# Outputs scaled in place of weights in four attention pairs, with an earlier second pair and two compose tiles

## The chip, the cores and the metric

One core of a Trainium2 chip runs the kernel. TensorE multiplies matrices, VectorE (DVE in the rows), ScalarE (ACT) and GpSimd (POOL) work on tiles, and SyncE (SP) issues most transfers. The metric is the device time of one launch in microseconds, less is better.

## The reference

Causal attention with a forget gate over 4 batches, 8 heads, 576 positions and 64 dimensions; then a dense feed-forward layer; then a layer in which each of the 2304 tokens goes to one of 8 experts. The change is in the attention and in the preparation of the dense layer's weights.

```python
scores = scale * np.matmul(q, k.transpose(0, 1, 3, 2))
log_f = np.log(np.clip(f, 0.0001, 1.0))
cum = np.cumsum(log_f, axis=-1)
decay = cum[:, :, :, None] - cum[:, :, None, :]
scores = np.where(causal, -1000000000.0, scores + decay)
scores = scores - np.max(scores, axis=-1, keepdims=True)
attn = np.exp(scores)
attn = attn / (np.sum(attn, axis=-1, keepdims=True) + 1e-09)
return np.matmul(attn, v).astype(np.float32)
...
h = x @ w_in
g = np.where(pos, h, np.where(neg, 0.0, (h + beta) ** 2 / (4.0 * beta)))
return (g @ w_out).astype(np.float32)
```

The dense layer's weights come in as 64-bit floats.

## The kernel before, in words

**Attention.** Two heads of a batch make a pair, and there are 16 pairs, 0 to 15. A pair has five units, taken in the order 4, 3, 2, 1, 0. Units 3 to 0 are blocks of 128 queries against the 512 to 128 keys they may see, both heads apart; unit 4 is the last 64 queries of both heads together against all 576 keys. For a unit, TensorE forms scores in a score bank (`SR` or `SRx`). In pairs 0 to 3 (`i < NSUM`) it also adds the running decay by products with `cum` or `parts`; in later pairs the decay comes as a mask `cm`, `cl`. Then for each head, in `head`:

- VectorE masks the scores, writes them to a tile `P` and takes the maximum (`tensor_tensor_reduce`, L588).
- ScalarE takes the exponential and its sum (L593), the sum going to a column of `st`.
- VectorE adds 1e-9 to the unit's sums (L598) and takes reciprocals (L600).
- GpSimd scales the weights in `P` by the reciprocal (L604).
- TensorE turns `P` in blocks of 128 into a bank `T` (L618; L616 for the last block), and ScalarE or VectorE copies it to `pt` or `pu` (L638, L636).

When both heads of units 3 to 0 are there, `weighted` multiplies them with the values into a bank `X` (L658), the value products, and ScalarE copies `X` to `xT` (L665). `weighted_last` does unit 4 (`U`, L711). `xT` goes to DRAM in `xs`. For the first four pairs its first 256 tokens also become the first block of the dense layer (`px0h`, `px0l`, in `first_block`), whose products can start when all four are there.

**Loads.** `load` brings the query and the key block of a pair (`rawq`, `rawk`, two tiles each) by four transfers on the SP queue, and VectorE turns each (L448). Pair 0 loads at once; every later pair waits for `sums_there`, the running sums of the forget gate.

**Weights.** The dense layer runs in two halves of the features. The weights of the first half (`wa`) come in 16 pieces of 128x512, a piece of `w_in` and one of `w_out` by turns. `float64_piece` makes each piece in a float32 tile `wx` and writes a high and a low part: an absolute value on ScalarE (L829), a maximum with a guard value (L830), three integer steps (L832, L834, L836) on VectorE, a cast on ScalarE (L840) and a subtraction on GpSimd (L841). One tile `wx` serves all pieces (`wx_b`), so a piece starts when the one before it is through.

**The dense layer** of the first half (`half0`) forms hidden banks (`hp`, L886), gates them on ScalarE, VectorE and GpSimd, and sums the second product in `accp` (L1020). It is mixed with attention from the end of pair 3 on: blocks 0 and 1 need batch 0 alone.

**Order.** The instructions of each engine are put in order ahead of time by a planner (`Order`), which lets the parts of the program run as coroutines against estimated costs. What was ready in its plan goes out by priority; the order is then fixed on each engine, and semaphores keep it right. Where TensorE has nothing in the plan during the first four pairs, `keep_warm` puts in products of `ident` with itself (`warm`, L735), which compute nothing that is used.

Of the kernel before, what the change touches and what calls it, by code (L numbers as in the profile page):

```python
# [18 lines left out]
P = 128  # L19
# [21 lines left out]
FIRST_WEIGHTS = [6000.0 + 2700.0 * n for n in range(5)] + [20500.0 + 5200.0 * n for n in range(11)]  # L41
PACE = 8500.0
WARM_FROM, WARM = 1500.0, 0.6

# [151 lines left out]
def act(n, fn, prio=5.0, more=0.0):  # L196
    return Use("ACT", 155 + n / 1.2 + more, fn, prio)
# [27 lines left out]
def kernel(  # L225
# [100 lines left out]
    for b in range(B):  # L326
        for n in range(b * S // TB, ((b + 1) * S - 1) // TB + 1):
            xs_ok[n].n += NPAIR
    raws, qkt, cms, vs, pt, pt4, xts = {}, {}, {}, {}, {}, {}, {}

# [60 lines left out]
    def load(i, n):  # L391
# [13 lines left out]
        g = yield (raw_b[n], 1)  # L405
        if i:
            yield sums_there
        t = yield dma(P * S * 6, lambda: put({"q": q, "k": k}[n], n), 4 if i else 0.5, k=4)
        raws[i, n] = (t, g)
# [109 lines left out]
    def unit(i, c, started):  # L519
# [47 lines left out]
        yield cm_ok[i, c]  # L567
        st = ap.tile([P, 8], F32, tag="st", name=f"st{i}_{c}", bufs=10)
        summed, scaled = Event(len(heads)), Event()
        left = Event(len(heads))  # L570
# [6 lines left out]
    def head(i, j, c, p, gp_, bank, st, summed, scaled, left):  # L577
# [8 lines left out]
        else:  # L586
# [4 lines left out]
        done(left)  # L591
        done(read_ok[i, c])
        yield act(w, lambda: nc.scalar.activation(pw, pw, AF.Exp, bias=st[:, n:n + 1], scale=-1.0,  # L593
                                                  accum_out=st[:, 2 + n:3 + n]), 1, 330)
        done(summed)
        if n == 0:
            yield summed
            yield Use("DVE", 150, lambda: nc.vector.tensor_scalar(  # L598
                st[:, 4:4 + k], st[:, 2:2 + k], 1e-9, None, ALU.add), 0)
            yield Use("DVE", 150, lambda: nc.vector.reciprocal(st[:, 6:6 + k], st[:, 4:4 + k]), 0)  # L600
            done(scaled)
        else:
            yield scaled
        yield pool1(w, lambda: nc.gpsimd.tensor_scalar(pw, pw, st[:, 6 + n:7 + n], 1.0, ALU.mult,  # L604
                                                       ALU.mult), 0)
        yield pt_ok[i, j]
# [33 lines left out]
        done(last_ok[i] if c == 4 else heads_ok[i])  # L640

    def weighted(i):

# [3 lines left out]
        xT = xts[i] = ap.tile([P, S], F32, tag="xT", name=f"xT{i}", bufs=2)  # L647
        go(weighted_last(i))
        vt, gr = vs[i]
        yield heads_ok[i]  # L650
# [12 lines left out]
        for j in range(2):  # L663
            give(pt_b, pt.pop((i, j))[1])
        yield act(512, lambda: nc.scalar.copy(xT[:, :512], X), 0)  # L665
        give(x_b, g)
# [74 lines left out]
    def attention():  # L741
# [23 lines left out]
    wr_b, wx_b, xl_b, t1_b, t2_b, x2_b, h_b, g_b, acc_b = (  # L765
        Buffers(2), Buffers(1), Buffers(1), Buffers(1), Buffers(1), Buffers(1), Buffers(1), Buffers(2), Buffers(0))

# [33 lines left out]
    def float64_weights(W, src_a, src_b, times, prio):  # L801
# [5 lines left out]
        for fc in range(NF):  # L807
            cs = slice(P * fc, P * fc + P)
            for src, hi, lo, ok in ((a[:, :, cs], ah[:, :, cs], al[:, :, cs], W.ok[0][fc]),
# [5 lines left out]
                n += 1  # L815

    def float64_piece(g, src, hi, lo, ok, name, prio):
        def put():
# [8 lines left out]

        x = fp.tile([P, DM], I32, tag="wx", name=name + "x", bufs=1)
        yield act(DM, lambda: nc.scalar.activation(f32(x), f32(hw), AF.Abs), prio)  # L829
        yield dve(DM, lambda: nc.vector.tensor_scalar(f32(x), f32(x), MIN64, None, ALU.max), prio,  # L830
                  True)
        yield dve(DM, lambda: nc.vector.tensor_scalar(  # L832
# [845 lines left out]

    W0 = Weights(wp1, "wa")
    with tc.manual_schedule():  # L1680
        go(attention())
        go(float64_weights(W0, w_in[:, :FH], w_out[:FH], FIRST_WEIGHTS, 0.8))
        go(phases())
        o.run()
        assert last_out.n == 0
# [38 lines left out]
```

## Time and profile before

| | |
|---|---|
| median of 3 runs | 861.24 us (859.62 to 863.11) |
| the profiled execution | 862.92 us, span 861.3 us |
| mean granted TensorE clock | 0.995 |
| busy: PE, DVE, ACT, POOL | 98%, 54%, 42%, 36% of the span |

The span runs from the first to the last instruction. Shares of busy time are means over the span. In the first ten of 40 slices DVE shows 5 to 9 tenths and in the last ones 1 to 2, so they are read by stretch.

### The profile page before, as it was taken

Reading aid. Unit: us, or ns where it says so; the run is one execution under the profiler, and the core shown is the slowest. Engines: PE = TensorE matmul, PEld = TensorE weight load, DVE = VectorE, ACT = ScalarE, POOL = GpSimd, SP = SyncE. Lnnn points to the kernel's source line nnn. Section 1 sums busy time; section 2 is a strip of 40 time slices with the busy share of each in tenths; the row PEclk is TensorE's granted clock in tenths of the full one; section 3 lists DMA queues with packets and bytes.
Section 4 is the critical chain, followed back from the end, with each engine's and each line's share of the span. In section 5 each row is a group of like instructions: output and inputs, shape, how many; then the busy total and the mean of one; then the engine's idle time right before and its main releaser. Section 6 shows DMA issues by size and latency. Waiting matters only on the chain.

```text
span 861.3 us, 14317 instructions
## 1 busy us (share of the span) xinstructions
PE 840.4 (98%) x5000; PEld 672.7 (78%) x5000; DVE 463.9 (54%) x1112; ACT 361.9 (42%) x845; POOL 306.4 (36%) x407
## 2 busy tenths in 40 slices
PE   9999998999999999999999999999999999999995
PEld 7665776787777798887788888888998888887684
DVE  6797977665555538766766344466544522212111
ACT  5677766665656635444344242323333212112110
POOL 3576876565455434544343122312210033000000
PEclk9999999999999999999999999999999999999998
DMA  7998666564323236225331135653431111721220
GB/s 139 184 183 182 167 159 145 139 135 108 113 67 118 78 103 134 74 75 171 117 127 49 73 123 159 189 191 123 147 123 73 50 50 50 263 103 50 98 74 25
DMA packets 152264, 101.91 MB, mean 118 GB/s; under 512 B 102866, under 2 KB 121810, under 8 KB 152192
## 3 DMA queue, kind: packets, MB, share of 16 engines
q1 hardware_dynamic: 149024, 96.22, 40.7%
q0 software_dynamic: 2832, 4.22, 1.7%
q8 instruction: 40, 0.66, 0.3%
q10 hardware_dynamic: 336, 0.56, 0.2%
q14 instruction: 32, 0.26, 0.1%
HBM read 76.86 MB, written 24.49 MB: 118 GB/s over the span
## 4 chain that ended last, share of the span: by engine, by line
PE 83%; DVE 7%; POOL 2%; issue 2%; DMA 2%; ACT 2%; SPq 0%; ACTq 0%; DVEq 0%; POOLq 0%
PE hm L886 12%; PE hr L886 12%; PE hp L886 9%; PE accp L1020 6%; PE accr L1020 6%; PE accBr L1020 6%; PE accm L1032 6%; PE accBm L1032 6%; PE SR L538 4%; PE T L618 4%; PE X L658 4%; PE gt L1236 1%; PE U L711 1%; PE SR L533 1%; PE T_None L618 1%
## 5 line engine op out<-in xcount | busy, mean ns | idle before, releaser
L908 POOL TENSOR_TENSOR glr<-gr,ghr 128x512 fp32r<-128x512 f32 x36 | 48.3, 1341 | 141.7 <-PE accBr L1020 69.1
L604 POOL TENSOR_SCALAR P<-P,st 128x512 f32<-128x512 f32 (+3 forms) x128 | 76.9, 615 | 38.8 <-DVE st L600 25.4
L886 PE MATMUL hr<-rx,wb 128*128 128x512 f32 (+1 forms) x384 | 90.1, 368 | 0.2 <-DVE rx L872 0.2
L886 PE MATMUL hm<-mx,wm 128*128 128x512 f32 (+1 forms) x336 | 87.0, 379 | 0.0
L593 ACT ACTIVATE P<-P,st 128x512 f32<-128x512 f32 (+3 forms) x128 | 71.4, 559 | 32.9 <-DVE st L588 31.8
L917 DVE SCALAR_TENSOR_TENSOR glm<-hm,ghm 128x512 fp32r<-128x512 f32 x36 | 24.8, 689 | 103.5 <-PE accBm L1032 68.4
L916 ACT ACTIVATE ghm<-hm 128x512 fp32r<-128x512 f32 x36 | 21.6, 599 | 132.9 <-PE accBm L1032 120.6
L886 PEld LDWEIGHTS hr<-rx,wb 128*128 128x128 f32 x384 | 65.5, 188 | 14.0 <-DVE rx L872 0.6
L886 PEld LDWEIGHTS hm<-mx,wm 128*128 128x128 f32 x336 | 61.0, 188 | 14.9 <-issue 3.4
L908 POOL TENSOR_TENSOR glp<-gp,ghp 128x512 fp32r<-128x512 f32 x36 | 49.8, 1383 | 55.1 <-ACT ghp L907 48.2
L1020 PE MATMUL accp<-ghp,wa 128*128 128x256 f32 (+1 forms) x384 | 68.8, 307 | 0.0
L588 DVE CUSTOM_DVE_ANT_0 P<-SR,cm 128x512 f32<-128x512 f32 (+3 forms) x96 | 45.1, 484 | 24.8 <-PE SR L538 22.5
L1020 PEld LDWEIGHTS accp<-ghp,wa 128*128 128x128 f32 x384 | 53.9, 190 | 5.3 <-issue 2.2
L618 PE MATMUL T<-ident,P 128*128 128x128 f32 x320 | 52.5, 278 | 3.5 <-POOL P L604 2.9
L638 ACT COPY pt<-T 128x512 f32<-128x512 f32 (+2 forms) x96 | 35.3, 391 | 35.9 <-PE T L618 35.2
L902 DVE SCALAR_TENSOR_TENSOR gr<-tr 128x512 f32<-128x512 f32 x36 | 25.9, 721 | 42.6 <-POOL glr L908 31.7
L618 PEld LDWEIGHTS T<-ident,P 128*128 128x128 f32 x320 | 36.7, 141 | 14.9 <-POOL P L604 6.5
L538 PE MATMUL SR<-kt,qt 64*128 64x384 f32 (+3 forms) x224 | 44.9, 478 | 3.0 <-DVE st L588 2.9
L1020 PE MATMUL accr<-ghr,wb 128*128 128x512 f32 (+1 forms) x160 | 47.0, 375 | 0.0
L1020 PE MATMUL accBr<-ghr,wb 128*128 128x512 f32 (+1 forms) x160 | 46.5, 372 | 0.0
L1032 PE MATMUL accm<-wm,ghm 128*128 128x512 f32 x144 | 46.2, 394 | 0.0
L1032 PE MATMUL accBm<-wm,ghm 128*128 128x512 f32 x144 | 45.8, 392 | 0.0
(345 smaller groups left out, 1864.3 us busy)
## 6 DMA issues: line engine op xcount, KB each, us to landing
cm<-rows SPq DMA_DIRECT2D x24, 256.0 KB, 4.3
rawq<-in_q_dram SPq DMA_DIRECT2D x64, 72.0 KB, 3.5
rawk<-in_k_dram SPq DMA_DIRECT2D x64, 72.0 KB, 3.2
xs<-xT SPq DMA_DIRECT2D x16, 288.0 KB, 2.2
x2n<-nat SPq DMA_DIRECT2D x18, 256.0 KB, 2.6
war<-in_moe_w_in_dram SPq DMA_DIRECT2D x8, 512.0 KB, 4.3
war<-in_moe_w_out_dram SPq DMA_DIRECT2D x8, 512.0 KB, 5.0
rawv<-in_v_dram SPq DMA_DIRECT2D x32, 128.0 KB, 2.6
```

Of the source, the lines that this page charges most:

```text
L538: nc.tensor.matmul(bank[:, j, :w], qt[p, P * c:P * c + P], kt[p, :w], start=True, stop=i >= NSUM)
L588: yield dve(w + 80, lambda: nc.vector.tensor_tensor_reduce(out=pv_, in0=so, in1=m, scale=-0.125, scalar=3e38, op0=ALU.add, op1=ALU.min, ac ...
L593: yield act(w, lambda: nc.scalar.activation(pw, pw, AF.Exp, bias=st[:, n:n + 1], scale=-1.0, accum_out=st[:, 2 + n:3 + n]), 1, 330)
L604: yield pool1(w, lambda: nc.gpsimd.tensor_scalar(pw, pw, st[:, 6 + n:7 + n], 1.0, ALU.mult, ALU.mult), 0)
L618: nc.tensor.transpose(T[:, P * n:P * n + P], p[:, P * kb:P * kb + P], ident)
L638: yield act(n, lambda: nc.scalar.copy(dh, src), 0)
L658: nc.tensor.matmul(X[D * j:D * j + D, P * kb:], vt[:, kb, j], pt[i, j][0][:, 512 * kb:512 * kb + 512 - P * kb], start=(kb == 0), stop=(kb ...
L886: nc.tensor.matmul(oo, a[:, c, cs], x[c], start=(ip == 0 and c == 0), stop=(ip == 2 and c == KC - 1))
L902: yield dve(n, lambda: nc.vector.scalar_tensor_tensor(g, t, 0.5, t, ALU.min, ALU.mult), 2)
L908: yield pool2(n, lambda: nc.gpsimd.tensor_tensor(gl, g, f32(gh), ALU.subtract), 1)
L1020: nc.tensor.matmul(acc[d][:, :w], b[:, fc, P * d:P * d + P], g, start=(fc == 0 and ip == 0 and (not narrow or d % 2 == 0)), stop=(fc == NF ...
L1032: nc.tensor.matmul(acc[a * (4 // na)], g[:, P * a:P * a + P], b[:, fc], start=(fc == 0 and ip == 0), stop=(fc == NF - 1 and ip == 2))
```

## The change

In pairs 0 to 3, units 3 to 0 are no longer scaled as weights. Their sums go to a tile `tot` of the pair (a column for each unit and head). When all eight are there, `shares` adds 1e-9, takes the reciprocals in one instruction each, and TensorE spreads them by eight products with `ident` into a bank `hR` that has the layout of `X`. `weighted` then lets ScalarE copy `hR` to `xT`, and VectorE multiplies `X` with it. Unit 4 and all later pairs stay as they were. Pair 1 loads when pair 0's key block has landed, ahead of the running sums. `wx_b` has two tiles until the first half's weights are made, the second of them in the pool of the attention; and nine of these pieces take their guard maximum on GpSimd.

```diff
-        if i:
+        if i == 1:
+            yield raw_ok[0, "k"]
+        elif i:
             yield sums_there
-        t = yield dma(P * S * 6, lambda: put({"q": q, "k": k}[n], n), 4 if i else 0.5, k=4)
+        t = yield dma(P * S * 6, lambda: put({"q": q, "k": k}[n], n),
+                      4 if i > 1 else 0.5, k=4)
...
+        late_sum = i < NSUM and c < 4
+        total = sums_of[i][:, c, n:n + 1] if late_sum else st[:, 2 + n:3 + n]
         yield act(w, lambda: nc.scalar.activation(pw, pw, AF.Exp, bias=st[:, n:n + 1], scale=-1.0,
-                                                  accum_out=st[:, 2 + n:3 + n]), 1, 330)
+                                                  accum_out=total), 1, 330)
         done(summed)
-        if n == 0:
+        if late_sum:
+            done(all_summed[i])
+        elif n == 0:
...
-        yield pool1(w, lambda: nc.gpsimd.tensor_scalar(pw, pw, st[:, 6 + n:7 + n], 1.0, ALU.mult,
-                                                       ALU.mult), 0)
+        if not late_sum:
+            yield pool1(w, lambda: nc.gpsimd.tensor_scalar(pw, pw, st[:, 6 + n:7 + n], 1.0,
+                                                           ALU.mult, ALU.mult), 0)
...
+    def shares(i):
+
+        yield all_summed[i]
+        tot = sums_of[i].rearrange("p c j -> p (c j)")
+        inv = ap.tile([P, 4, 2], F32, tag="inv", name=f"inv{i}", bufs=2)
+        yield Use("DVE", 150, lambda: nc.vector.tensor_scalar(tot, tot, 1e-9, None, ALU.add), 0)
+        yield Use("DVE", 150, lambda: nc.vector.reciprocal(inv.rearrange("p c j -> p (c j)"), tot), 0)
+        gh_ = yield (h_b, 1)
+        R = hidden_bank(f"R{i}", 0)
+
+        def spread():
+            for c in range(4):
+                for j in range(2):
+                    nc.tensor.matmul(R[D * j:D * j + D, P * c:P * c + P],
+                                     inv[:, c, j:j + 1].to_broadcast([P, D]), ident,
+                                     start=True, stop=True)
+        yield Use("PE", mm(P, 8), spread, 0.9)
+        share[i].t = R, gh_
+        done(share[i])
...
-        yield act(512, lambda: nc.scalar.copy(xT[:, :512], X), 0)
+        if i < NSUM:
+            yield share[i]
+            R, gh_ = share[i].t
+            yield act(512, lambda: nc.scalar.copy(xT[:, :512], R), 0)
+            give(h_b, gh_)
+            yield dve(512, lambda: nc.vector.tensor_tensor(xT[:, :512], X, xT[:, :512], ALU.mult), 0)
+        else:
+            yield act(512, lambda: nc.scalar.copy(xT[:, :512], X), 0)
...
-    wr_b, wx_b, xl_b, t1_b, t2_b, x2_b, h_b, g_b, acc_b = (
-        Buffers(2), Buffers(1), Buffers(1), Buffers(1), Buffers(1), Buffers(1), Buffers(1), Buffers(2), Buffers(0))
+        Buffers(2), Buffers(2), Buffers(1), Buffers(1), Buffers(1), Buffers(1), Buffers(1), Buffers(2), Buffers(0))
...
-        x = fp.tile([P, DM], I32, tag="wx", name=name + "x", bufs=1)
+        x = (ap if gx[0] else fp).tile([P, DM], I32, tag="wx", name=name + "x", bufs=1)
         yield act(DM, lambda: nc.scalar.activation(f32(x), f32(hw), AF.Abs), prio)
-        yield dve(DM, lambda: nc.vector.tensor_scalar(f32(x), f32(x), MIN64, None, ALU.max), prio,
-                  True)
+        if name == "wa" and len(early_max) < NMAX:
+            early_max.append(0)
+            yield Use("POOL", 1500, lambda: nc.gpsimd.tensor_scalar(
+                f32(x), f32(x), MIN64, None, ALU.max), prio)
```

On the SP queue, from the first transfers on, before (`rawq0` and `rawk0` are pair 0's blocks, `war` a weight piece, `rawv` values):

```order
L400 DMA rawq0_135<-in_q_dram 32x18x32 x4
L400 DMA rawk0_144<-in_k_dram 32x18x32 x4
L820 DMA war_160<-in_moe_w_in_dram 128x4x128
L820 DMA war_176<-in_moe_w_out_dram 128x512
L373 DMA rows_79<-cum_88 32x576
```

and of now:

```order
L402 DMA rawq0_135<-in_q_dram 32x18x32 x4
L402 DMA rawk0_144<-in_k_dram 32x18x32 x4
L863 DMA war_160<-in_moe_w_in_dram 128x4x128
L402 DMA rawq1_166<-in_q_dram 32x18x32 x4
L402 DMA rawk1_184<-in_k_dram 32x18x32 x4
L375 DMA rows_79<-cum_88 32x576
```

Pair 1's two blocks moved ahead of the running sums `rows` and of the second weight piece; before, they stand behind the sums and all values of two pairs.

On TensorE, ahead of pair 1's value products `X`, before (`T` are turned weights of pair 1, `SR` and `SRx` scores of pair 2):

```order
L618 MATMUL T_000_663<-ident,P_00_592 128x128
L735 MATMUL warm_503<-ident 128x128
L538 MATMUL SRx<-kt_110,qt_109 128x384 x2
L618 MATMUL T_100_673<-ident,P_10_593 128x128
L560 MATMUL SRx<-parts,picks 128x384 x2
L538 MATMUL SR<-kt_110,qt_109 128x256 x2
L658 MATMUL X_687<-pt_0_367,rawv_212 64x512
```

and of now:

```order
L630 MATMUL T_000_609<-ident,P_00_551 128x128
L565 MATMUL SRx<-parts,picks 128x512 x2
L543 MATMUL SR<-kt_110,qt_109 128x384 x2
L630 MATMUL T_100_634<-ident,P_10_552 128x128
L565 MATMUL SR<-parts,picks 128x384 x2
L667 MATMUL hR_645<-ident,inv_619 64x128 x8
L543 MATMUL SRx<-kt_110,qt_109 128x256 x2
L692 MATMUL X_654<-pt_0_443,rawv_222 64x512
```

The eight spreading products came in two rows ahead of `X`, and the warming product is gone. They wait for `inv`, VectorE's reciprocals.

On TensorE, between the value products of pairs 5 and 6, before (`hp_6` holds the hidden bank of the last two feature chunks of block 0):

```order
L618 MATMUL T_120_1770<-ident,P_12_1703 128x128 x3
L538 MATMUL SR<-kt_945,qt_944 128x128 x2
L533 MATMUL SR<-kt_1227,qz_86 128x288 x2
L886 MATMUL hp_6_1647<-px0h,wa_96 128x256 x4
L886 MATMUL hp_6_1647<-px0l,wa_96 128x256 x4
L886 MATMUL hp_6_1647<-px0h,wa_97 128x256 x4
L618 MATMUL T_010_1823<-ident,P_01_1753 128x128 x2
L618 MATMUL T_110_1839<-ident,P_11_1754 128x128 x2
L538 MATMUL SR<-kt_1227,qt_1226 128x512 x2
```

and of now, from the same pair's last scores on (`hp_2` here belongs to block 1):

```order
L543 MATMUL SR<-kt_921,qt_920 128x128 x2
L752 MATMUL U_1797<-pu_1558,rawv_1444 64x64 x10
L630 MATMUL T_020_1839<-ident,P_02_1747 128x128 x3
L538 MATMUL SR<-kt_1269,qz_86 128x288 x2
L934 MATMUL hp_2_1802<-px1h,wa_96 128x256 x4
L934 MATMUL hp_2_1802<-px1l,wa_96 128x256 x4
L934 MATMUL hp_2_1802<-px1h,wa_97 128x256 x4
L630 MATMUL T_120_1861<-ident,P_12_1748 128x128 x3
L630 MATMUL T_010_1878<-ident,P_01_1781 128x128 x2
L934 MATMUL hp_2_1802<-px1h,wa_96 128x256 x4
```

Block 0's last hidden products have moved ahead of pair 5's value products, and block 1's stand here; 72 products of the first layer lie between the two pairs' value products in place of 12. Over the whole order the warming products go from 88 to 67.

## Rows read from the trace of the kernel before

**Rows 1.** The page: busy time by engine, and the granted clock in 40 slices.
```profile
PE 840.4 (98%) x5000; PEld 672.7 (78%) x5000; DVE 463.9 (54%) x1112; ACT 361.9 (42%) x845; POOL 306.4 (36%) x407
...
PEclk9999999999999999999999999999999999999998
```

**Rows 2.** Windows: stretch, its length, busy us by engine, clock, DMA share, GB/s.
```profile
8.00:34.00 26.00, 25.72 (x191) 19.32 (x190) 19.69 (x53) 17.39 (x40) 10.53 (x17) 1.00 0.81 164
34.00:88.00 54.00, 49.29 (x365) 31.36 (x366) 46.32 (x144) 39.85 (x111) 33.36 (x51) 1.00 0.91 185
88.00:126.00 38.00, 38.00 (x293) 30.51 (x291) 32.56 (x87) 25.49 (x68) 30.46 (x43) 1.00 0.65 161
126.00:146.00 20.00, 15.99 (x109) 11.10 (x106) 15.93 (x43) 12.96 (x34) 13.62 (x21) 0.91 0.58 142
146.00:300.00 154.00, 153.85 (x1226) 120.58 (x1225) 90.23 (x293) 92.80 (x250) 81.55 (x146) 1.00 0.44 111
300.00:861.00 561.00, 551.07 (x2790) 453.33 (x2789) 256.04 (x487) 171.90 (x344) 132.71 (x117) 1.00 0.34 108
```

**Rows 3.** The same windows for the warming products alone (L735): PE, PEld.
```profile
8.00:34.00 26.00, 13.00 (x95) 11.48 (x93) 1.00 0.81 164
34.00:88.00 54.00, 7.88 (x47) 6.55 (x46) 1.00 0.91 185
```

**Rows 4.** Waits of TensorE, 8 to 88 us: total, times, longest.
```profile
PE T L618 <- POOL P L604: 2.9, 6, 0.8
```

**Rows 5.** Timeline of VectorE, 29 to 36 us: start, duration, in brackets idle before.
```profile
29.53 0.77 DVE L448 STREAM_TRANSPOSE kt<-rawk 128x576 f32<-128x576 f32 x1
...
34.95 0.78 DVE L448 STREAM_TRANSPOSE qt<-rawq 128x576 f32<-128x576 f32 x1 [2.73 <-DMA rawq<-in_q_dram]
```

**Rows 6.** Timeline of GpSimd, 118 to 146 us: last steps of two weight pieces.
```profile
124.46 1.28 POOL L841 TENSOR_TENSOR wa<-wax,wa 128x512 fp32r<-128x512 f32 x1 [2.55 <-ACT wa L840]
...
132.58 1.27 POOL L841 TENSOR_TENSOR wa<-wax,wa 128x512 fp32r<-128x512 f32 x1 [0.47 <-ACT wa L840]
```

**Rows 7.** Timeline of TensorE, 126 to 138 us.
```profile
132.78 2.29 PE L533 MATMUL SR<-kt,qz 128*128 128x288 f32 x4 [0.99 <-DVE st L588]
134.45 1.47 PE L886 MATMUL hp<-px0h,wa 128*128 128x256 f32 x4
```

**Rows 8.** Timeline of TensorE, 114 to 122 us.
```profile
115.68 1.14 PE L533 MATMUL SR<-kt,qz 128*128 128x288 f32 x4
...
121.13 0.72 PE L886 MATMUL hp<-px0h,wa 128*128 128x256 f32 x4
```

**Rows 9.** Instructions by line on GpSimd, 8 to 88 us: busy us, mean ns.
```profile
L604 POOL TENSOR_SCALAR P<-P,st 128x512 f32<-128x512 f32 (+3 forms) x32 | 20.4, 651 | 9.3 <-DVE st L600 8.7 <-DVE st L598 0.5
L841 POOL TENSOR_TENSOR wa<-wax,wa 128x512 fp32r<-128x512 f32 x9 | 11.8, 1310 | 12.4 <-ACT wa L840 12.3
```

**Rows 10.** Instructions by line and form on VectorE, 8 to 88 us.
```profile
L834 DVE SCALAR_TENSOR_TENSOR wax<-war,wax 128x512 int32<-128x512 int32 x10 | 7.1, 712 | 0.1
...
L598 DVE TENSOR_SCALAR st<-st 128x2 f32<-128x2 f32 x17 | 6.7, 393 | 1.1 <-ACT P L593 1.1
...
L830 DVE TENSOR_SCALAR wax<-wax 128x512 f32<-128x512 f32 x10 | 4.5, 448 | 0.7 <-ACT wax L829 0.7
...
L600 DVE RECIPROCAL st<-st 128x2 f32<-128x2 f32 x17 | 2.5, 149 | 0.0
```

**Rows 11.** The chain of waits, 14 to 36 us: start, us, what (records).
```profile
16.87 0.64 PE warm L735 x4
...
21.71 1.34 PE warm L735 x12
23.05 0.11 PE T_None L616
```

**Rows 12.** Timeline of VectorE, 39 to 41 us.
```profile
39.77 0.65 DVE L598 TENSOR_SCALAR st<-st 128x2 f32<-128x2 f32 x1
```

**Rows 13.** Timeline of GpSimd, 39 to 41 us.
```profile
39.65 0.74 POOL L694 TENSOR_TENSOR px0l<-xT,px0h 128x256 fp32r<-128x256 f32 x1
```

More of the change, by code (lines that the diff above doesn't have):

```diff
@@ L42 @@
 PACE = 8500.0
+NMAX = 9
 WARM_FROM, WARM = 1500.0, 0.6
@@ L328 @@
             xs_ok[n].n += NPAIR
+    all_summed, share, sums_of = [Event(8) for _ in range(NP)], [Event() for _ in range(NP)], {}
     raws, qkt, cms, vs, pt, pt4, xts = {}, {}, {}, {}, {}, {}, {}
@@ L568, in unit @@
         st = ap.tile([P, 8], F32, tag="st", name=f"st{i}_{c}", bufs=10)
+        if i < NSUM and c == 3:
+            sums_of[i] = ap.tile([P, 4, 2], F32, tag="tot", name=f"tot{i}", bufs=2)
         summed, scaled = Event(len(heads)), Event()
@@ L648, in weighted @@
         go(weighted_last(i))
+        if i < NSUM:
+            go(shares(i))
         vt, gr = vs[i]
@@ L664, in weighted @@
             give(pt_b, pt.pop((i, j))[1])
-        yield act(512, lambda: nc.scalar.copy(xT[:, :512], X), 0)
+        if i < NSUM:
+            yield share[i]
[5 more added lines that the diff above has]
+            yield act(512, lambda: nc.scalar.copy(xT[:, :512], X), 0)
         give(x_b, g)
@@ L815, in float64_weights @@
                 n += 1
+    early_max = []
     def float64_piece(g, src, hi, lo, ok, name, prio):
@@ L825, in float64_piece @@
         lw, hw = w[:, :, 0], w[:, :, 1]
-        x = fp.tile([P, DM], I32, tag="wx", name=name + "x", bufs=1)
+        x = (ap if gx[0] else fp).tile([P, DM], I32, tag="wx", name=name + "x", bufs=1)
         yield act(DM, lambda: nc.scalar.activation(f32(x), f32(hw), AF.Abs), prio)
-        yield dve(DM, lambda: nc.vector.tensor_scalar(f32(x), f32(x), MIN64, None, ALU.max), prio,
-                  True)
+        if name == "wa" and len(early_max) < NMAX:
+            early_max.append(0)
+            yield Use("POOL", 1500, lambda: nc.gpsimd.tensor_scalar(
+                f32(x), f32(x), MIN64, None, ALU.max), prio)
+        else:
+            yield dve(DM, lambda: nc.vector.tensor_scalar(f32(x), f32(x), MIN64, None, ALU.max),
+                      prio, True)
         yield dve(DM, lambda: nc.vector.tensor_scalar(
@@ L1679, with one_tile @@
     W0 = Weights(wp1, "wa")
+    def one_tile():
+        for ok in W0.ok[0] + W0.ok[1]:
+            yield ok
+        yield (wx_b, ((1,),))
     with tc.manual_schedule():
@@ L1682 @@
         go(float64_weights(W0, w_in[:, :FH], w_out[:FH], FIRST_WEIGHTS, 0.8))
+        go(one_tile())
         go(phases())
```

## The prediction

> **What bounds the kernel now.** I read the page's first two parts first. TensorE is busy 98% of the span and its granted clock reads 9 (full, 2.4 GHz) in nearly every slice [rows 1]. So the span is TensorE's instruction stream, and a change can only shorten it by taking instructions out of that stream or by closing gaps in it. Next I cut the span into stretches that end where the character of the stream changes [rows 2]. From 146 to 300 us, where attention pairs and the first layer are mixed, TensorE lacks 0.15 us of 154: nothing is to be had there. From 88 to 126 us it lacks nothing. Three stretches have room. From 8 to 34 us it lacks 0.28 us, from 34 to 88 us 4.71 us, and from 126 to 146 us 4.01 us, at a mean clock of 0.91. The gaps after 300 us (9.9 us) lie behind the change.
>
> Busy is not the same as useful. The third view is the same stretches for the warming products alone [rows 3]. They fill 13.0 us between 8 and 34 us and 7.9 us between 34 and 88 us. They compute nothing; they stand where the planner expected TensorE to have nothing ready. The first 88 us thus hold about 21 us of filler after 8 us, besides 5.0 us of true gaps. What ends the gaps is mostly one thing: a transposition of weights waits for GpSimd's scaling, 2.9 us in six places [rows 4]. After 88 us there are no warming products, because work of the first layer fills in.
>
> Why that early stretch is thin can be seen on VectorE. The key block of the second pair is turned only at 29.53 us, and at 34.95 us the queue has stood 2.73 us for the query block of a later pair [rows 5], so the early units of attention wait for blocks of other pairs as well as for their own.
>
> The stretch from 126 to 146 us has another cause. The products of the first layer's last two feature chunks need the last pieces of its weights, and those come one every eight microseconds: the last step of the fourteenth begins at 124.46 us and of the fifteenth at 132.58 us [rows 6]. The hidden product that needs the fifteenth piece starts at 134.45 us [rows 7]. The order of before shows the consequence: between the value products of the sixth and seventh pair stand only 12 products of the first layer. In this stretch the clock then halved: the product of 288 columns takes 2.29 us and the next group 1.47 us [rows 7], against 1.14 and 0.72 us for the same kinds before the drop [rows 8]. That is 1.15 and 0.75 us more; neighbours overlap in these durations, so I count 1.5 us for the clock of 1.2 GHz. Right before it fell, TensorE had stood 0.99 us for VectorE [rows 7].
>
> **The change part by part.**
>
> *Outputs scaled instead of weights.* It removes 32 scalings from GpSimd (8 in each of four pairs), 20.4 us of its time at a mean of 0.651 [rows 9]. It removes 16 additions and 16 reciprocals from VectorE, at 0.393 and 0.149 us, 8.7 us [rows 10], and adds 4 of each (1.2 us at 0.15, since the long mean comes from waits) and 4 products of 128x512, each about 0.71 us by the nearest two-operand row [rows 10], 2.8 us. Neither engine is the bound, so these sums cost or give nothing by themselves; they matter through the waits they end.
>
> What counts is on TensorE: 8 small products in each of four pairs that spread the reciprocals over 64 rows, 32 in all. The trace has no such product. Its nearest row is a warming product, also 128 rows by 128 columns in float32: 1.34 us for six in a row (12 records), 0.22 each; in a run of two it is 0.32 [rows 11]. From below, a single turned block of 128 columns advances the stream by 0.11 us [rows 11]. I take 0.22, because the eight stand in one run: 32 x 0.22 = **+7.0 us**, between +3.5 and +10.2. The planner books half of that, so TensorE will run behind the plan there, which makes others late less often.
>
> *Second pair early, scaling gone: fewer warming products.* The order has 88 warming products before and 67 now, 28 of them in both at the very start. So 21 go. At 0.22 to 0.32 us [rows 11] I take 0.27: **-5.7 us**, between -4.6 and -6.7. Fourteen of those left stand in one row of pair 0: VectorE now turns the second pair's blocks ahead of pair 0's first maximum, and its key block has to land first.
>
> *Gaps up to 88 us.* Of 5.0 us, the 2.9 behind GpSimd's scaling go [rows 4], since a weight tile is now turned straight after its exponential. New ones appear: TensorE stands at the eight small products until VectorE has the reciprocal, four times, before it can go on to the value products. I take **-2.5 us**; the bounds are -5.0 (all gaps gone) and +3.0 (1.5 us lost per pair on top of half of the old ones).
>
> *Two compose tiles and nine maxima on GpSimd.* A piece of the first weights needs a float32 tile in which it is composed, and before there was one; the next piece's first step waits for the last step of the one before. With two, pieces overlap. A maximum leaves VectorE nine times, 0.448 us each [rows 10], 4.0 us. On GpSimd the nearest rows are the scalings, 0.651 us over all their widths, and above them the two-operand subtraction of the full width at 1.31 [rows 9]: I take 0.8, 7.2 us, and 6 to 12 us come to an engine that has just lost 20.4. In the order of now the sixteenth piece is composed a pair earlier, and between the value products of the sixth and seventh pair stand 72 products of the first layer in place of 12. So the gaps of 4.0 us and the 1.5 us of the slow clock from 126 to 146 us should go. The work that fills them isn't new; it is taken from later, where the stream is full. VectorE has seven pieces to do in the two pairs after the first layer's start and may make TensorE wait a little: **-5.0 us** of 5.5, bounds -5.5 and 0.
>
> **Sum.** 7.0 - 5.7 - 2.5 - 5.0 = -6.2 us. The profiled execution took 862.92 us (span 861.3), 1.7 above the median of the runs shown, 861.24. That execution would come to 856.7 us, and a median run to **855.0 us**, 0.7% less.
>
> **A rule weighed against a row.** A VectorE addition on two numbers a partition starts at 39.77 us and takes 0.65 us, where a reciprocal of the same size takes 0.15 [rows 10]; it ends as a GpSimd subtraction that began at 39.65 us ends [rows 12, 13]. So some VectorE operations stand until GpSimd is through, and each maximum moved there may hold VectorE up for its length. The Trainium skill (SBUF — State Buffer, Who interferes with whom) states this as a lock: an operation of VectorE in a two-port mode and one of GpSimd exclude each other for a whole instruction, which speaks against putting work on GpSimd. By that rule, the trace agrees: 0.65 us in the row named.
>
> **The rivals.**
>
> *The late stall only moves.* With the weights there, pairs 4 and 5 get more first-layer work and seven weight pieces at once. VectorE was busy 32.6 of 38 us from 88 to 126 us [rows 2], so TensorE could wait there as it now does at 126. Then that term is 0 and the sum -1.2 us: 860.0. For it: VectorE's share of 86%. Against: no gap at all in that stretch before. Chance 0.20.
>
> *Small products cheap, all gaps close.* At 0.11 us each and with the early gaps gone, 3.5 - 5.7 - 5.0 - 5.5 = -12.7 us: 848.5. For it: GpSimd leaves the path to the turned blocks. Against: the products are of the kind that costs 0.22. Chance 0.12.
>
> *Slower: TensorE stands for the reciprocals.* The small products come ahead of the value products in TensorE's queue, and VectorE's reciprocal stands behind turns of later pairs' blocks, which wait for transfers; [rows 5] shows such a stand of 2.73 us. Everything behind is held: next pair's scores and turned blocks. At 2.7 us in each of four pairs the gap term is 4 x 2.7 = +10.8 in place of -2.5, and the sum is +7.1: 868.3. It decides from about 0.9 us a pair, where the whole gain is gone (-6.2 + 2.5 + 3.7 = 0). Against: 24 warming products stand ahead of the first small products besides pair 0's own work, so TensorE comes to them late. Chance 0.10.
>
> *Held by GpSimd.* Nine maxima of 0.8 us hold VectorE for 7.2 us, all of it reaching TensorE: +1.0 us, 862.2. Against: GpSimd as a whole does 20.4 - 7.2 = 13.2 us less beside VectorE. Chance 0.03.
>
> **How the numbers follow.** My forecast has 0.55. Its own range is -9 to -3 us, 852 to 858. Half a per cent, 4.3 us, is about what a measurement of this kernel can tell from no change; four fifths of the forecast's chance lie beyond it. Faster: 0.44 + 0.12 = 0.56. Same: 0.11 + 0.20 + 0.03 = 0.34. Slower: 0.10. For 8 in 10 I go from 849, near the cheap rival, to 862, past the rival of the moved stall; the slower one and a bit of the cheap one stay outside.
>
> **What the profile after would show.** The small products: about 1.8 us for eight. The first layer's first product between 84 and 89 us; before, it comes where the third stretch of [rows 2] begins, and it need not be much earlier, since 7.0 us were added ahead of it. TensorE's gaps from 8 us to that product 2 to 3 us, none ended by a scaling of pairs 0 to 3 other than the last rows' units. Fifteenth weight piece by about 110 us, and no slow clock near 130 us. The prediction is wrong if the small products cost over 0.3 us each, if TensorE's longest waits are for the reciprocal, or if a gap of some microseconds opens in pairs 4 to 6 in place of the one closed.

## The result and the profile after

The changed kernel takes 872.02 us (median of 4 runs, 869.4 to 875.25) where the one before took 860.43 beside it: a ratio of 1.0127, 95% interval [1.0095, 1.0158]. It is slower by 11 to 12 us; the forecast was 6 us faster. The profiled execution took 869.40 us (span 867.7), the fastest of its runs.

The first two parts of the page of the kernel after:

```profile
PE 840.6 (97%) x5022; PEld 671.3 (77%) x5022; DVE 464.1 (53%) x1083; ACT 361.0 (42%) x845; POOL 298.0 (34%) x384
...
PEclk9999999999999998999999999999999999999998
```

TensorE is as busy as before in microseconds [rows 1]; what grew is the time in which it stands. Apart from the last slice, which is low in both kernels, the one low digit of the clock stands two fifths into the span, behind the stretch on which the prediction spent its words. The windows of the kernel after, cut as in [rows 2] up to 300 us, and two more behind it:

```profile
8.00:34.00 26.00, 25.39 (x190) 18.21 (x188) 20.32 (x53) 16.91 (x40) 11.22 (x12) 1.00 1.01 180
34.00:88.00 54.00, 47.26 (x389) 30.76 (x387) 46.60 (x121) 40.22 (x113) 29.50 (x35) 1.00 0.82 178
88.00:126.00 38.00, 35.28 (x276) 29.17 (x275) 35.68 (x81) 23.81 (x59) 29.45 (x39) 1.00 0.64 165
126.00:146.00 20.00, 20.00 (x163) 15.96 (x161) 10.43 (x38) 11.84 (x33) 11.42 (x21) 1.00 0.57 113
146.00:300.00 154.00, 153.76 (x1224) 120.90 (x1223) 88.76 (x292) 90.76 (x247) 80.03 (x144) 1.00 0.45 111
...
300.00:346.00 46.00, 41.80 (x279) 33.05 (x278) 21.60 (x55) 23.68 (x53) 14.08 (x28) 0.93 0.38 108
346.00:480.00 134.00, 130.29 (x563) 104.84 (x563) 92.98 (x126) 55.59 (x94) 58.27 (x40) 1.00 0.32 102
```

The late stall is closed: 126 to 146 us is full, at full clock. But from 34 to 88 us TensorE lacks 6.74 us (4.71 before), from 88 to 126 us 2.72 (0 before), and from 300 to 480 us 4.20 + 3.71 = 7.91 us, where the kernel before lacks 1.2. The mean clock from 300 to 346 us is 0.93. The warming products are fewer, as forecast [rows 3]:

```profile
8.00:34.00 26.00, 9.59 (x71) 8.46 (x69) 1.00 1.01 180
34.00:88.00 54.00, 4.58 (x28) 3.77 (x27) 1.00 0.82 178
```

**The end of attention.** Timeline of TensorE, kernel after:

```profile
321.95 2.37 PE L692 MATMUL X<-pt,rawv 128*64 128x512 f32 x16
324.25 1.22 PE L1068 MATMUL accp<-ghp,wa 128*128 128x256 f32 x8
...
329.99 0.28 PE L1068 MATMUL accp<-glp,wa 128*128 128x256 f32 x1
331.46 1.01 PE L934 MATMUL hp<-px,wa 128*128 128x512 f32 x2 [1.19 <-ACT px L919]
333.00 0.50 PE L934 MATMUL hp<-px,wa 128*128 128x512 f32 x1 [0.52 <-ACT px L919]
334.98 10.22 PE L934 MATMUL hp<-px,wa 128*128 128x512 f32 x32 [1.47 <-ACT px L919]
```

The same place in the kernel before:

```profile
310.35 2.38 PE L658 MATMUL X<-pt,rawv 128*64 128x512 f32 x16
312.66 0.74 PE L886 MATMUL hp<-px4h,wa 128*128 128x256 f32 x4
...
331.79 8.56 PE L886 MATMUL hp<-px,wa 128*128 128x512 f32 x36
```

Behind the last value products the attention outputs go to DRAM, come back as the first wide block `px` and are cast on ScalarE; I call this the hand-over. Before, 156 products of the first layer (counted in the order) stood behind the last `X` and kept TensorE busy for 19 us, and the block was there in time. After, 48 stand there, 6.0 us; the other 108, some 13 us, were spent in pairs 4 to 15, and the last `X` comes 11.6 us later. TensorE waits three times for a cast, 3.18 us, and from within the third wait on the clock reads 1.2 GHz for 6.8 us: 32 products take 10.22 us, where 36 took 8.56.

**The early gaps.** ScalarE's waits, kernel after, 8 to 110 us (in the kernel before it stands not once for `war`):

```profile
ACT wax L872 <- DMA war<-in_moe_w_in_dram: 4.6, 5, 2.5
ACT wax L872 <- DMA war<-in_moe_w_out_dram: 4.5, 3, 2.2
```

And one of these places, in the timelines of ScalarE, VectorE, GpSimd and TensorE of the kernel after; the first row and the last three are used further down:

```profile
32.69 1.09 PE L667 MATMUL hR<-ident,inv 128*64 128x128 f32 x16
...
41.76 0.67 ACT L872 ACTIVATE wax<-war 128x512 f32<-128x512 f32 x1 [2.47 <-DMA war<-in_moe_w_in_dram]
42.33 0.57 ACT L702 COPY xT<-hR 128x512 f32<-128x512 f32 x1
42.80 0.59 ACT L650 COPY pt<-T 128x512 f32<-128x512 f32 x1
...
44.10 1.49 DVE L880 TENSOR_SCALAR wax<-wax 128x512 int32<-128x512 int32 x1 [0.27 <-POOL wax L875]
45.51 0.28 DVE L595 CUSTOM_DVE_ANT_0 P<-SRx,past 128x128 f32<-128x128 f32 x1
...
44.03 1.27 POOL L889 TENSOR_TENSOR wa<-wax,wa 128x512 fp32r<-128x512 f32 x1
...
43.44 0.55 PE L630 MATMUL T<-ident,P 128*128 128x128 f32 x3 [0.85 <-ACT pt L650]
45.85 1.13 PE L543 MATMUL SRx<-kt,qt 64*128 64x512 f32 x4 [1.30 <-DVE st L595]
...
60.79 1.46 POOL L889 TENSOR_TENSOR wa<-wax,wa 128x512 fp32r<-128x512 f32 x1
...
61.25 1.55 DVE L882 SCALAR_TENSOR_TENSOR wax<-war,wax 128x512 int32<-128x512 int32 x1
...
63.74 0.41 PE L630 MATMUL T<-ident,P 128*128 128x128 f32 x2 [0.85 <-DVE xT L758]
```

ScalarE has nothing to do but wait 2.47 us for a weight piece, and the copies of `hR` and `pt` stand in its queue behind it; TensorE waits 0.85 us for that copy. Then VectorE's integer step takes 1.49 us beside a GpSimd subtraction, and the next mask with maximum comes late: 1.30 us more. With one compose tile the absolute value waited for the last step of the piece before; by then its own transfer had landed. With two tiles it may go as soon as the plan reckons the transfer landed, and the plan is too early by up to 2.5 us.

The second tile does one thing more. With one, the subtraction on GpSimd ends a piece before the next begins, and in the six kernels with one tile (before, e1, e3, e4, e10, e12 below) no integer step of a first-half piece runs beside such a subtraction. With two, 12 of the 48 do in the changed kernel, at a mean of 1.13 us, where the steps with GpSimd idle beside them take 0.64. The last three rows show one: the step at 61.25 us takes 1.55 us, and TensorE waits 0.85 us for VectorE's copy behind it.

### The profile page after: what moved, and what is told of

The parts are those of the page before. It is cut to its first block, busy times and chain, and to the rows that moved or that the text cites. A ratio compares the mean times of both kernels' runs of the same rounds, so it can differ in the third digit from the quotient of the medians.

```text
span 867.7 us, 14283 instructions
## 1 busy us (share of the span) xinstructions
PE 840.6 (97%) x5022; PEld 671.3 (77%) x5022; DVE 464.1 (53%) x1083; ACT 361.0 (42%) x845; POOL 298.0 (34%) x384
## 4 chain that ended last, share of the span: by engine, by line
PE 78%; DVE 9%; DMA 5%; issue 2%; ACT 2%; POOL 2%; SPq 1%; ACTq 0%; POOLq 0%; DVEq 0%
PE hm L934 12%; PE hr L934 12%; PE hp L934 7%; PE accp L1068 6%; PE accr L1068 6%; PE accBr L1068 6%; PE accm L1080 6%; PE accBm L1080 6%; PE SR L543 4%; PE X L692 3%; PE T L630 3%; DMA war<-in_moe_w_in_dram 2%; PE gt L1284 1%; DVE gp L950 1%; PE SR L538 1%
## 5 line engine op out<-in xcount | busy, mean ns | idle before, releaser
L616 POOL TENSOR_SCALAR P<-P,st 128x512 f32<-128x512 f32 (+3 forms) x96 | 56.2, 597 | 37.5 <-DVE st L611 19.4
```

## The experiments

The experiments were planned on two of these costs.

**Theory 1.** The second tile costs in two places: ScalarE's queue stands for transfers early, and the first layer's work is spent before the hand-over, which it had covered. **Rival.** The nine maxima do it, by what they do to VectorE. **Second rival.** The scaling or the early pair do it.

The changed kernel is taken apart by four edits (the lines that decide; code that only serves them is left out). S takes the scaled outputs out, L the early pair, M the maxima off GpSimd, T the second tile:

```diff
S -        late_sum = i < NSUM and c < 4
S +        late_sum = False
L -        if i == 1:
L -            yield raw_ok[0, "k"]
L -        elif i:
L +        if i:
M -NMAX = 9
M +NMAX = 0
T -        Buffers(2), Buffers(2), Buffers(1), Buffers(1), Buffers(1), Buffers(1), Buffers(1), Buffers(2), Buffers(0))
T +        Buffers(2), Buffers(1), Buffers(1), Buffers(1), Buffers(1), Buffers(1), Buffers(1), Buffers(2), Buffers(0))
T -        go(one_tile())
```

The runs in one table. Stand: ScalarE's waits for `war` up to 110 us. Idle: length of the stretch less TensorE's busy time. Half: time at a granted 1.2 GHz ahead of the last product. Behind X: first-layer products behind the last value products in the order. One profile each, not always of a middling run (that of e7 is the slowest of six, 877.0 us, that of after the fastest of four); the ratio to the kernel before is over all runs.

| kernel | us | ratio, 95% interval | stand | idle 34-100 | 100-146 | 300-480 | half | behind X |
|---|---|---|---|---|---|---|---|---|
| before | 861 | | 0 | 4.7 | 4.0 | 1.2 | 3.4 | 156 |
| after | 872.0 | 1.0127 [1.0095, 1.0158] | 9.1 | 8.9 | 0.6 | 7.9 | 6.8 | 48 |
| e1 = M, T | 867.3 | 1.0065 [1.0047, 1.0084] | 1.0 | 1.5 | 7.7 | 5.8 | 3.4 | 144 |
| e2 = S, L | 876.0 | 1.0171 [1.0137, 1.0205] | 1.4 | 5.9 | 3.0 | 5.6 | 23.9 | 96 |
| e3 = L, M, T | 856.8 | 0.9946 [0.9929, 0.9963] | 0.9 | 3.2 | 2.6 | 1.2 | 0 | 144 |
| e4 = S, M, T | 863.1 | 1.0011 [0.9997, 1.0024] | 0 | 3.0 | 7.2 | 1.2 | 10.2 | 144 |
| e5 = M | 868.1 | 1.0080 [1.0062, 1.0098] | 8.9 | 6.0 | 1.9 | 2.5 | 6.8 | 72 |
| e7 | 872.2 | 1.0113 [1.0089, 1.0136] | 10.7 | 9.7 | 1.1 | 10.1 | 10.2 | 48 |
| e8 = L, M | 888.0 | 1.0313 [1.0292, 1.0333] | 16.0 | 5.8 | 3.0 | 9.6 | 13.7 | 24 |
| e9 = S, L, M | 873.8 | 1.0135 [1.0114, 1.0157] | 13.5 | 7.2 | 0.5 | 4.1 | 10.2 | 108 |
| e10 = S, L, T | 872.5 | 1.0126 [1.0106, 1.0147] | 0 | 4.9 | 5.4 | 1.0 | 10.2 | 156 |
| e11 | 876.0 | 1.0175 [1.0154, 1.0195] | 8.8 | 7.3 | 0.6 | 11.4 | 17.1 | 96 |
| e12 | 871.8 | 1.0118 [1.0096, 1.0140] | 0.9 | 3.1 | 2.6 | 10.9 | 17.1 | 144 |
| e13 | 860.7 | 0.9990 [0.9976, 1.0004] | 0 | 2.7 | 4.7 | 3.1 | 10.2 | 120 |
| e14 | 860.8 | 0.9981 [0.9969, 0.9993] | 0 | 2.2 | 7.0 | 1.2 | 3.4 | 144 |
| e15 | 862.0 | 0.9997 [0.9984, 1.0009] | 0 | 3.7 | 4.8 | 1.5 | 6.8 | 144 |
| e16 | 859.2 | 0.9964 [0.9949, 0.9979] | 0 | 4.3 | 3.2 | 1.2 | 3.4 | 144 |

**The parts one by one (e1 to e4).**

> The change without its third part: one compose tile, all guard maxima on VectorE; outputs are still scaled and the second pair still loads early. In this order 144 products of the first layer's first half stand behind the last pair's value products (48 in the changed kernel, 156 before). Theory 1, first-layer work used up too early: the gap behind the last pair's value products (3.2 us of idle, 6.8 us of half clock in the changed kernel) is gone; a gap near the sixth and seventh pair comes back in part, since only 36 products stand there; time 858 to 864 us. Theory 2, the cost is in the first 100 us (spreading products, waits of the chain): the time stays at 868 to 874 us.

> The kernel before with the third part alone: two compose tiles and nine maxima on GpSimd; weights scaled as before, the second pair loaded as before. 96 products of the first half stand behind the last value products. Theory 1: the gap near the seventh pair closes, and 96 products of 0.12 us are 11.5 us of cover for a hand-over that takes about 7 to 11 us in the changed kernel, so idle there under 1.5 us and no long half clock; time 853 to 862 us, not slower than before. Theory 2, GpSimd and the tiles themselves cost (VectorE held by GpSimd): slower than before by 4 us or more, with added idle of TensorE in the first 126 us.

> The kernel before with the scaled outputs alone (spreading products, no early pair, one compose tile). 144 products stand behind the last value products, 36 between those of pairs 5 and 6. Theory 1: no gap at the hand-over; first product of the first layer at 86 to 89 us; time 856 to 863 us. Theory 2, the new chain in the first four pairs costs: that first product at 91 us or later and the time at 865 us or more.

> The kernel before with the early load of the second pair alone. 72 warming products in place of 88, 144 products behind the last value products. Theory 1: no gap at the hand-over; fewer warming products (16 x 0.27 = 4 us) should show as an earlier first product of the first layer, 84 to 87 us, and the time at 856 to 861 us. Theory 2: turning the second pair's blocks ahead of pair 0's first maximum costs more than it gives; first product no earlier than 88 us, time 861 to 866 us.

e1 missed what either theory gave. The second rival falls: the scaling alone is faster by 0.5%, the early pair alone changes nothing clear of noise (though e4's 863.1 us lies in the range given for its loss), and the weight part alone costs 15 us, with 23.9 us at half clock, the most of all. The parts don't add up, though: scaling and pair together (e1) are slower by 0.65%, with 6 us of gaps from 300 to 480 us though 144 products stand behind the last `X`. That run speaks against Theory 1 as the whole story.

**The weight part split (e5, e8, e9, e10).**

> The changed kernel with all guard maxima back on VectorE: scaled outputs, early second pair, two compose tiles. In the changed kernel the nine maxima take GpSimd 1.49 us each and the integer step behind them on VectorE grew from 0.49 to 0.71 us. If they make a good part of the loss: 862 to 867 us. If the two tiles make it, by ScalarE's queue standing for weight transfers (9.1 us up to 110 us in the changed kernel, none in the one before) and by the hand-over: 869 to 874 us, with ScalarE still standing 8 us or more for transfers there. Its order leaves 72 first-layer products behind the last value products, 24 more than the changed kernel, so the gap at the hand-over should be 0 to 2 us in place of 3.2.

> Scaled outputs and two compose tiles; the second pair loads as before and the maxima stay on VectorE. Its order leaves 24 first-layer products (some 3 us) behind the last value products, where the hand-over takes about 9 us. If uncovered hand-overs are what two tiles cost: a gap there of 5 to 7 us plus a half clock of 3 us behind it, warming products 103 in place of 66 (some 8 us), so 868 to 876 us against 856.8 for scaling alone. If the tiles cost nothing by themselves: 855 to 860 us, and no gap over 2 us at the hand-over.

> Only the second compose tile is added to the kernel before; scaled weights, load order and maxima stay as before. With both halves of the weight part the time was 876.0 us. If the tiles make the loss, because weights come early, first-layer products are spent early and the plan is redrawn: 870 to 877 us, first-layer products behind the last value products 108 in place of 156. If the maxima on GpSimd make it: 859 to 865 us. From the order: 27 more warming products than before, at 0.22 us 5.9 us, so with no other loss 866 or so, which would speak for a loss of both.

> Only the nine maxima are moved to GpSimd, with one compose tile and nothing else of the change. If the maxima make the loss of the weight part, by holding VectorE or by coming late on GpSimd behind the scalings: 870 to 877 us, with longer gaps on TensorE from 88 to 146 us where the weights come. If the tiles make it: 858 to 864 us. Its order keeps 156 first-layer products behind the last value products, so the hand-over to the wide blocks should show no gap in either case.

e5 (868.1 us) fell between its two ranges: ScalarE stands 8.9 us as expected of two tiles, and the maxima are worth 4 us within the change. Both halves cost 11 to 12 us alone, so neither theory has all of it. They cost in different places. With the second tile and the maxima on VectorE, ScalarE stands (e9's largest row, and e8's):

```profile
ACT wax L859 <- DMA war<-in_moe_w_in_dram: 10.3, 5, 4.0
```

```profile
ACT wax L870 <- DMA war<-in_moe_w_in_dram: 11.0, 6, 3.8
```

In e2, which has both halves, it stands only 1.4 us. In e9 TensorE also runs 28.0 us of warming products behind 8 us, 7.1 more than in the kernel before.

With the maxima alone ScalarE doesn't stand; TensorE waits longer for GpSimd's scalings (waits of TensorE over the whole of e10; before, the 2.9 us of [rows 4] are all of them):

```profile
PE T L626 <- POOL P L612: 8.5, 8, 1.8
```

That the maxima hold these scalings up is not shown: three of the eight waits, 3.7 us, come after the last maximum, which starts at 90.5 us. Much of e10's loss lies outside the columns of the table: TensorE lacks 4.5 us from 146 to 300 us (0.15 before) and 2.2 us from 8 to 34 us (0.28).

In e8, 24 products are left behind the last `X`. The hand-over shows the gap that was expected, and the time, 888 us, is the worst of all and beyond the 868 to 876 us expected (timeline of TensorE, e8):

```profile
344.34 0.80 PE L932 MATMUL hp<-px,wa 128*128 128x512 f32 x1 [3.70 <-ACT px L917]
346.13 1.42 PE L932 MATMUL hp<-px,wa 128*128 128x512 f32 x2 [0.99 <-ACT px L917]
```

**The hand-over (e7, e11, e12).** e7 puts warming products into the hand-over of the changed kernel, e11 holds first-layer work back for it, and e12 uncovers it in the good kernel e3:

```diff
e7  +            for _ in range(16):
e7  +                yield Use("PE", mm(P, 2), lambda: nc.tensor.matmul(
e7  +                    X[:, :P], ident, ident, start=True, stop=True), 9, after=0.0)
e11 +                    if self is half0 and n == NARROW - 1 and u == (0, 1):
e11 +                        yield pv_ok[NP - 1]
...
e12      def load_wide(src, w, ok, name, ev):
e12          yield ok
e12 +        yield narrow_done
```

> The changed kernel with 16 products of ident with itself put ahead of the first product of the wide block, at 0.22 us 3.5 us of work that stands where TensorE idles 3.2 us for the casts. If the half clock behind the hand-over (6.8 us of it, 3.4 us lost) comes from these gaps, it goes and the time falls to 868 to 869.5 us, with no wait for a cast of the wide block's tokens over 0.3 us. If the half clock has another cause, or the wait only moves on: 871 to 874 us.

> The changed kernel in which the second products of the last narrow block are held back in the plan until the last value products are out: 96 first-layer products stand behind them in place of 48, and nothing ahead of the last two pairs moves. If the loss at 330 to 341 us is the uncovered hand-over: the gaps of 3.2 us and the half clock behind them (6.8 us, 3.4 us lost) go, with no new gap over 1 us in the last two pairs: 864 to 867.5 us. If the last pairs need that work to be full: the gap opens there and the time stays at 870 to 873 us.

> The kernel with scaled outputs alone (856.8 us), in which the loads of the first wide block are put in the plan behind the last products of the narrow blocks, so that the hand-over is no longer covered; up to the last value products every engine's order is the same. If an uncovered hand-over costs what the changed kernel shows: gaps of 3 to 6 us on TensorE before the wide block's first products and a half clock of 3.4 to 10 us behind them, 861 to 868 us. If the hand-over is free, or its loss is made up later: 855 to 859 us.

(`narrow_done` is set by the last narrow block's last product.) e12 is the clean one: up to the last value products every engine's order is that of e3, and it costs 15 us more (1.0118 against 0.9946). Windows of e12, then TensorE's row at the gap; in e3 the stretch from 300 to 346 us is full and the next lacks 1.16 us:

```profile
300.00:346.00 46.00, 38.55 (x276) 33.59 (x275) 23.35 (x50) 20.54 (x43) 13.80 (x25) 0.89 0.53 123
346.00:480.00 134.00, 130.54 (x551) 104.91 (x550) 83.34 (x114) 52.60 (x87) 53.12 (x38) 0.97 0.29 94
```

```profile
335.98 1.84 PE L935 MATMUL hp<-px,wa 128*128 128x512 f32 x3 [7.16 <-ACT px L920]
```

So the gap itself (7.2 us) is half of the price. The rest is 17.1 us of half clock, 10.2 of them from inside the gap on and 6.8 from inside a wait of 2.2 us at 432 us; together they cost up to 8.5 us, and the gaps from 346 to 480 us 2.3 us more. That is more than I expected, but on the side of Theory 1. The gap made here is more than twice the 3.18 us of the changed kernel.

e7 and e11 missed what Theory 1 gave. In e7 (872.2 us, as when the wait only moves on) the profile shows no gain, though it is of the slowest execution, 877.0 us: TensorE waits 5.51 us a little later, for ScalarE, which stands 7.21 us for a transfer of the second half's weights (`wbr`; timelines of TensorE and ScalarE):

```profile
348.73 3.78 PE L934 MATMUL hp<-px,wa 128*128 128x512 f32 x8 [5.51 <-ACT tp L946]
...
346.32 0.66 ACT L872 ACTIVATE wbx<-wbr 128x512 f32<-128x512 f32 x1 [7.21 <-DMA wbr<-in_moe_w_in_dram]
```

In e11 the work held back leaves a hole where it had stood (timeline of TensorE):

```profile
318.81 0.68 PE L630 MATMUL T<-ident,P 128*128 128x128 f32 x2 [2.86 <-POOL P L616]
```

The stream of the last pairs needs that work too. Handing it back at the end didn't mend the loss.

**The transfers (e13 to e16).** The plan reckons a weight piece as landed later by `d`: 3.0 us in e13, 3.5 in e15, both on the whole change; 3.5 in e14 and 4.0 in e16, with edit M:

```diff
+        if name == "wa":
+            yield o.now + d
         gx = yield (wx_b, 1)
```

> The changed kernel in which the plan reckons 3 us more until a weight piece of the first half has landed, so that the absolute value on ScalarE is put later in its queue; both tiles and all nine maxima stay. If the early loss comes from ScalarE standing for transfers: it stands 2 us or less for them up to 110 us, TensorE's gaps from 34 to 100 us fall from 8.9 to 5 us or less; and as this order leaves 120 first-layer products behind the last value products, the hand-over shows no gap over 0.5 us: 858 to 864 us. If the tiles or maxima cost by what they do to VectorE and GpSimd: gaps of 7 us or more stay up to 100 us, and 866 to 873 us.

> Scaled outputs, early second pair, two tiles, all maxima on VectorE, and 3.5 us more reckoned until a weight piece has landed. 144 first-layer products stand behind the last value products and 66 warming products in the order. If nothing of the loss was due to the tiles but ScalarE's stands and the uncovered hand-over: ScalarE stands under 1 us for the weights, no gap over 1 us at the hand-over, and 855 to 861 us. If two tiles load VectorE in the pairs before the first layer by themselves: gaps of 5 us or more from 34 to 126 us and 862 to 868 us.

> The same as the run before it, with the nine maxima on GpSimd, that is the whole change with 3.5 us more reckoned for the landing; 144 products behind the last value products, 61 warming products. If the maxima cost by holding VectorE's integer steps: those steps have a mean of 0.7 us or more in place of 0.5, and the time is 3 to 6 us above the run before it. If they cost nothing once ScalarE doesn't stand: within 2 us of it, and by 5 fewer warming products perhaps 1 us less.

> As the first of these three, with 4.0 in place of 3.5 us. Its order is nearest to that of scaling alone, with the early second pair and 7 fewer warming products: 144 products behind the last value products, 48 before the sixth pair's. By the sum of idle, warming and half clock 852 to 858 us, at least as good as scaling alone (856.8 us). If a longer reckoned landing only brings the late stall at 126 to 146 us back in full (4 us): 859 to 862 us.

e13 keeps every part of the change and takes back all of the loss, by this one edit. ScalarE never stands for the first weights, only 2 of the 48 integer steps run beside a subtraction of GpSimd in place of 12, and the windows show it:

```profile
34.00:100.00 66.00, 63.26 (x510) 44.33 (x510) 55.87 (x158) 49.67 (x140) 42.54 (x52) 1.00 0.81 180
100.00:146.00 46.00, 41.30 (x308) 28.97 (x305) 39.89 (x107) 31.73 (x82) 35.56 (x49) 1.00 0.59 146
```

From 34 to 100 us 2.74 us are lacking in place of 8.87. But the late stall is back, 4.7 us, as in every order in which the weights are not early (2.6 to 7.7 us); and two waits of 1.0 and 1.3 us stay at the hand-over, which I had not expected with 120 products ahead, and 10.2 us of half clock stand near 15 us, where no other kernel but e2 and e14 has any. e14 and e15 put the maxima at about 1 us there, their intervals overlapping: VectorE's integer steps have a mean of 0.56 and 0.69 us in e15, not the 0.7 and 0.97 of the changed kernel. e16 is the best form with two tiles, but missed its 852 to 858 us and came out as if the late stall were back (3.2 us of it are); scaling alone, 856.8 us, is the fastest kernel of the study and beats both.

## Why the prediction was wrong

**Small products.** Forecast +7.0, bounds +3.5 and +10.2. The eight at 32.69 us in the timeline above (16 records) took 1.1 us, not 1.8, and all 32 took 4.4 us, the first of these three groups by line of the kernel after:

```profile
L667 PE MATMUL hR<-ident,inv 128*64 128x128 f32 x64 | 4.4, 279 | 0.0
...
L875 POOL TENSOR_SCALAR wax<-wax 128x512 f32<-128x512 f32 x9 | 13.4, 1487 | 18.9 <-ACT wax L872 18.9
...
L880 DVE TENSOR_SCALAR wax<-wax 128x512 int32<-128x512 int32 x16 | 11.4, 712 | 1.7 <-POOL wax L875 1.7
```

A product that writes 64 rows went at 0.14 us, so the lower row was the nearer one. No product stood for a reciprocal (0.0 in the row); that rival is out.

**Warming products.** Forecast -5.7; 20.88 us became 14.17, and 0.49 stand behind 88 us: -6.2. Right.

**Gaps up to 88 us.** Forecast -2.5, bounds -5.0 and +3.0. They went from 4.99 to 7.35 us, +2.4. What was to go went: of the 2.9 us of waits for GpSimd's scaling none is left (the first, 0.45 us, comes at 91.55 us). Of what came, gaps of 1.41 and 0.85 us end behind stands of ScalarE, which were not weighed at all, and gaps of 1.30, 0.85 and 1.28 us (up to 45.85, 63.74 and 77.13 us) behind integer steps of VectorE that ran beside a GpSimd subtraction. The prediction had such a hold as a rival, at 0.03, but from the maxima; it was the second tile that put the steps there. e1, which has the scaling and the pair without the tiles and the maxima, lacks 1.5 us from 34 to 100 us, so the sign was right without the weight part.

**Two tiles and maxima.** Forecast -5.0. The stall of 4.0 us went, with 3.4 us at half clock (1.7 lost), but 2.7 us opened from 88 to 126 us: -3.0. That is partly the rival of the stall that only moves. Of the maxima the size was wrong: GpSimd takes 1.49 us for one, where I took 0.8 and had the row of 1.31 as its upper bound (the second row); the plan itself books 1.5 us, in the diff of the change. VectorE's step L880 (the third) rose from a mean of 0.49 to 0.71 us. The step at 44.10 us ended 0.29 us after the subtraction on GpSimd that had begun just before it. The Trainium skill (SBUF — State Buffer, Who interferes with whom) has this as an exclusive lock between such a step of VectorE and GpSimd; by that rule, the trace agrees, 1.49 us in place of 0.49.

**The step that failed.** "The gaps after 300 us (9.9 us) lie behind the change", and with it "it is taken from later, where the stream is full". The later stream was full because this work was in it. Taken from there, it uncovered the hand-over. The prediction put this term at nothing; it came to +6.7 us of idle from 300 to 480 us, and 6.8 us of half clock, up to 3.4 us lost (a part of it lies in the gap). That is 10.1 of the 13.9 us between forecast and the sum below. Of the idle time 3.18 us are the waits at the hand-over itself; waits near 395 and 428 us add 3.7 us, where the like ones of the kernel before take 0.9, and e1, with its hand-over covered, has 3.0, so these are not shown to belong to it. e12 shows that an uncovering, if a wider one, costs 15 us in a kernel that is the same up to there. Of the prediction's three signs of being wrong, only the third came in part (2.7 us from 88 to 126 us); none looked behind 300 us.

With these sizes the sum is 4.4 - 6.2 + 2.4 - 3.0 + 6.7 + 3.4 = +7.7 us. The profiled executions differ by 6.5 (869.40 - 862.92); the last product starts 8.1 us later, and the stretch behind it is 1.6 us shorter. The median run of after lost some 5 us more against that of before than the profiled one did, which no trace here shows.

**What stays open.** Where the loss was, and that the early release of weight pieces sets it off, is shown by e13 to e16: four orders with two tiles at 859 to 862 us, where the same two kernels without the later landing (after, e5) take 872 and 868. How it divides between ScalarE's stands, VectorE's held steps and the hand-over is not: e13 mends all three, the hand-over in part, and e11, which was to mend the hand-over alone, opened another gap. The price of a part by itself is no property of the part, since each order is planned anew: the maxima cost 11 us alone, 4 within the change, about 1 in e15. Why the maxima alone cost 11 us, and why e1 has 5.8 us of gaps behind 300 us with 144 products there, no run shows.

## What to carry to other kernels

Before work is moved into a gap, ask what it covered where it stood: a full stretch with filler in it is not a stretch with nothing to lose. A buffer that ends a wait also ends what the wait was good for; here the single tile kept an in-order queue from standing at a transfer that had not landed, and VectorE's steps on one piece apart from GpSimd's step on the piece before, so look at what the freed instruction waits for next and at who is queued behind it. When an order is planned from estimates, test a part by its effect on the whole order, and don't add the parts.

## What the runs showed of the hardware

Idle time on TensorE was often paid for twice. From within the hand-over's gap of 7.16 us in e12 the clock read 1.2 GHz for 10.2 us, from within the 3.18 us of the changed kernel for 6.8, and in e4 for 6.8 us right behind a gap of 2.46 us at 113 us. In e3, whose longest gap behind 88 us is 1.2 us, it never fell before the end; nor did it in e14 between 112 and 144 us amid five gaps of 0.4 to 1.7 us, though it did in the kernel before within the 0.99 us of [rows 7], behind gaps of 0.4 and 0.7 us.

A transfer of 512 KB landed in 4.3 to 4.8 us as a median early in the changed kernel, but near the hand-over one kept ScalarE standing 7.2 us in one execution (e7) and 2.9 us in another (the kernel after) at the same place of the order.

An integer step of VectorE beside a subtraction of GpSimd took 1.13 us as a mean of 12 in the changed kernel and 1.30 us of 9 in e5, against 0.64 and 0.57 us with GpSimd idle.
